# Sliding-window attention and a token-mixing MLP: PSUM as eight single banks, each with reads of its own

## The chip, the cores and the metric

The kernel runs on one core of a Trainium2 chip. The metric is device time in microseconds (us), the median of three runs. The core has a matrix engine (TensorE, PE in the profile; PEld is its weight load), a vector engine (VectorE, DVE), a scalar engine (ScalarE, ACT), GpSimd (POOL) and a sync engine (SP). Each works through its own list of instructions in order, and waits at an instruction until what it needs is there. PE writes its results only to PSUM, a small memory of eight banks, each 128 partitions by 512 fp32 numbers; ACT and DVE read PSUM and write SBUF, the working memory. In this kernel POOL starts nearly all input transfers, SP and ACT the output transfers.

## The reference

Eight batches, eight heads, 576 tokens, head size 64. Attention with a linear distance penalty, over the last 128 tokens, then a token-mixing MLP on the concatenated heads:

```python
scores = scale * np.matmul(q, k.transpose(0, 1, 3, 2))
mask = (rel >= 0) & (rel < 128)
scores = np.where(mask, scores - slopes * np.abs(rel), -1e9)
attn = softmax(scores)
x = np.matmul(attn, v)                      # then heads side by side: (8, 576, 512)
wq = x @ w_q; wk = x @ w_k                  # 512 -> 64
W_tok = einsum('bsd,btd->bst', wq, wk) / 8
mixed = einsum('bst,btd->bsd', W_tok, x)
out = np.maximum(mixed, 0) @ w_out          # 512 -> 512
```

## The kernel before

The program is a list of named operations. A long string, `ORDER`, gives their order and the engine of each (`:P` PE, `:A` ACT, `:D` DVE, `:G` POOL, `:S` SP) and, for PE, the PSUM place. It is written out by hand or by a tool outside the file; nothing decides about the order at run time. Every engine gets the operations that name it, in the order of the string.

The operations of one batch `b`, in the order in which data passes through them:

- `Lq`, `Lk`, `Lv`, `Lt` load q, k, v and the last 64 tokens (POOL). `LF` loads the first pieces of batch 0 in fp32 (ACT, SP).
- `TQ`, `TK`, `TT`, `TJ`, `TF` transpose q and k on PE into PSUM; `ETQ`, `ETK`, `ETT`, `EJ`, `EF` copy the results to the tile `qkT` (L252 on ACT, L254 on DVE).
- `QK b.g.u` makes the scores of key block `g` (0 to 3) and head half `u`: four heads, 1024 numbers in each partition, which is two banks. `EXP b.g.u` (L657, ACT) takes the exponential of the 1024 into the tile `pt`. `MUL b.g` (L672, DVE) multiplies the 2048 numbers of both halves with the penalty and mask factors in `bias`.
- `PV b.t` multiplies with v for query block `t`, with the row sums in a 65th column for each head, for all eight heads into two banks. `RC` (L723, DVE) takes the reciprocals of the eight sums, `X` (L733, DVE) scales the 512 numbers into the tile `x`. Block 4 holds the last 64 tokens and takes one bank (L720, L727).
- `XT b.i` transposes two blocks of `x` (L243), eight transposes of 128x128 into one bank, and `EXT` copies the 1024 fp16 numbers to `xT`. `XTT`, `EXTT` do the last 64 tokens.
- For each pair of batches: `WQ`, `WK`, `WT` (products with w_q and w_k), `G` (wk times x), `MX 0..4` (the mixed tokens, two banks each), `RM` and `RMT` (relu, L886 on ACT, L888 on DVE), `OUT` (product with w_out, four matmuls of 512 columns), `EO` (copy to the staging tile `osb`), `DO` (store).
- `WM` are matmuls on zeros, put where PE would pause; `WARM` has their numbers. `wmc` and `bias` make the factors at the start, `zeros`, `ones` and `pads` clear tiles.

PSUM is four tiles `pair0` to `pair3` of two banks. An operation of two banks takes a whole pair (`:P2`), one of one bank half a pair (`:P21`). The function `apart` declares that operations on the two banks of one pair don't depend on each other; an operation that reads both banks at once holds both until it is done.

Of the kernel before, what the change touches and what calls it, by code (L numbers as in the profile page):

```python
# [8 lines left out]
FP32 = mybir.dt.float32  # L9
# [8 lines left out]
H = 8  # L18
# [20 lines left out]
LOGB = ()  # L39

LAST = (7, 3)

PAIRED = 9
# [3 lines left out]
WARM = (6, 9, 1, 1, 2, 3,)  # L47

ORDER = """
warm:D LF0.0.0.0:A LF0.0.1.0:S ones.2:D iota:G LF0.0.1.1:A LF0.1.0.0:S ident:G LF0.0.0.1:A  # L50
zeros:D LF0.1.0.1:S Lv2.4:G ones.1:D Lq0.2:G pads:D Lk0.2:G wmc:D WM.0:P31 TF0.0.0:P00 Lk0.1:G
ones.3:D bias:A Lq1.0:G ones.0:D TF0.0.1:P01 idh:D Lk1.0:G TF0.1.1:P10 EF0.0.1:D Lk1.1:G
TF0.1.0:P11 EF0.1.1:D Lv0.0:G EF0.0.0:A EF0.1.0:A Lk1.2:G Lk1.3:G WM.1:P31 TJ0.2.1:P1
QK0.0.1:P0 QK0.0.0:P2 EJ0.2.1:D Lv0.1:G TJ0.2.0:P30 EXP0.0.0:A TJ0.1.1:P1 EJ0.2.0:D Lk0.3:G
EXP0.0.1:A QK0.2.1:P3 EJ0.1.1:D QK0.2.0:P2 QK0.1.1:P1 EXP0.2.1:A MUL0.0:D TQ1:P0 EXP0.2.0:A
Lv0.2:G QK0.1.0:P3 Lt0:G ETQ1:D EXP0.1.0:A TK1.0:P2 ETK1.0:D EXP0.1.1:A Lv1.0:G MUL0.2:D
WM.2:P01 QK1.1.1:P2 QK1.1.0:P3 QK1.0.1:P1 EXP1.1.1:A Lv1.1:G QK1.0.0:P0 MUL0.1:D EXP1.1.0:A
Lq2.0:G TK1.1:P2 ETK1.1:D EXP1.0.1:A Lk2.3:G PV0.0:P3 QK1.2.1:P2 RC0.0:D Lk2.2:G X0.0:D
EXP1.0.0:A PV0.1:P1 MUL1.1:D PV0.2:P3 Lv1.2:G EXP1.2.1:A QK1.2.0:P0 Lv0.3:G RC0.1:D EXP1.2.0:A
X0.1:D TT0:P2 RC0.2:D Lv1.3:G TJ0.3.1:P1 X0.2:D ETT0:A XT0.0:P00 ETT1:A MUL1.0:D Lk2.0:G  # L60
EJ0.3.1:A WM.3:P01 QK1.3.0:P2 Lv0.4:G EXP1.3.0:A EXT0.0:D PV1.0:P1 QK0.3.1:P3 RC1.0:D PV1.1:P0
X1.0:D EXP0.3.1:A QK0.3.0:P2 MUL1.2:D QK1.3.1:P1 EXP0.3.0:A TQ2:P3 Lk2.1:G RC1.1:D EXP1.3.1:A
MUL0.3:D Lv1.4:G ETQ2:A WM.4:P21 TK2.1:P1 X1.1:D Lt1:G ETK2.1:D PV1.2:P2 XT1.0:P00 RC1.2:D
PV0.3:P3 X1.2:D Lw1:G QK2.2.1:P1 MUL1.3:D Lk3.1:G EXP2.2.1:A Lw0:G RC0.3:D WM.5:P01 PV1.3:P2
EXT1.0:A X0.3:D Lq3.0:G PV0.4:P01 RC1.3:D X1.3:D TK2.0:P3 QK2.2.0:P1 Lv2.0:G RC0.4:D PV1.4:P00
ETK2.0:D EXP2.2.0:A XT1.1:P20 Lk3.0:G RC1.4:D X0.4:D QK2.0.0:P3 EXT1.1:D XT0.1:P21 EXP2.0.0:A
Lk3.3:G QK2.0.1:P1 X1.4:D EXT0.1:D QK2.1.1:P0 Lk3.2:G EXP2.0.1:A TT2:P3 QK2.1.0:P2 ETT2:D
Lv2.1:G EXP2.1.1:A ETT3:D WK0:P10 MUL2.0:D Lv2.2:G EXP2.1.0:A XTT0:P0 QK2.3.0:P3 EXTT0:D
WQ0:P11 Lv2.3:G EWK0:A MUL2.1:D EXP2.3.0:A QK2.3.1:P0 TQ3:P2 Lq4.0:G MUL2.2:D EXP2.3.1:A Lwo0:G
WT0:P10 ETQ3:D PV2.0:P0 EWT0:A Lwo1:G TK3.0:P3 ETK3.0:A G0:P10 RC2.0:D Lk4.1:G X2.0:D MUL2.3:D  # L70
# [12 lines left out]
TK4.1:P3 OUT0.3:P21 EXP5.0.0:A Lk6.0:G ETK4.1:D TT4:P1 EO0.0:D EO0.3:A Lq6.02:G XTT2:P3
QK5.1.1:P0 ETT5:D ETT4:A OUT1.0:P20 EXTT2:D Lk6.2:G EXP5.1.1:A MUL4.1:D PV4.0:P3 Lk6.1:G
QK4.2.0:P1 EO1.0:A QK4.2.1:P0 RC4.0:D WK2:P21 EXP4.2.0:A X4.0:D Lv5.1:G MUL5.1:D OUT1.4:P20
EXP4.2.1:A Lk6.3:G PV4.1:P1 MUL5.0:D EWK2:A Lq6.01:G EO1.4:A TK5.1:P0 QK4.3.0:P3 Lv4.3:G
WQ2:P21 RC4.1:D EXP4.3.0:A X4.1:D Lq6.00:G ETK5.1:D WT2:P20 EWQ2:A QK4.3.1:P3 MUL4.2:D EWT2:A
Lq6.03:G QK5.2.0:P0 PV5.0:P1 EXP4.3.1:A G2:P20 Lk7.0:G RC5.0:D X5.0:D EXP5.2.0:A Lv4.4:G
MUL4.3:D QK5.2.1:P3 XT4.0:P21 EG2:A Lk7.1:G PV4.2:P0 EXP5.2.1:A EXT4.0:D MX2.3:P1 Lq7.02:G
RC4.2:D MX2.2:P2 RM2.3:A X4.2:D TK6.1:P3 Lt3:G ETK6.1:D TK6.0:P0 RM2.2:A PV5.1:P1 ETK6.0:D  # L90
MX2.0:P3 RC5.1:D PV4.3:P0 Lq7.01:G X5.1:D RM2.0:A QK5.3.1:P2 RC4.3:D TQ6:P1 Lv5.2:G X4.3:D
# [68 lines left out]
def kernel(  # L160
# [45 lines left out]
    def one(bank):  # L206
        return pairs[bank[0]][:, bank[1], :]
# [867 lines left out]
```

## Time and profile before

| | before |
|---|---|
| median of 3 runs | 137.24 us (136.44 to 137.88) |
| span of the profiled execution, first to last instruction | 135.4 us |
| PE busy | 122.8 us (91%), 2174 matmuls |
| DVE busy | 114.0 us (84%), 197 instructions |
| ACT busy | 107.3 us (79%), 145 instructions |
| POOL busy | 86.3 us (64%), 108 instructions |
| granted TensorE clock | 1.000 |

The profile gives the profiled execution's span, not its device time; the median lies 1.84 us above the span. Times of a row are microseconds from the span's start. On ACT and DVE an instruction's end overlaps the next one's start, so that the time from start to start in an unbroken sequence, called the step below, is shorter than an instruction's duration. A row of the timeline that covers several instructions (x12) gives their time together. In the view of waits a row names who waited, for whom, how long in all, how often and the longest.

### The profile page before, as it was taken

The page shows a single profiled execution, that of the slowest core. Times are in us where ns is not written, and L with a number is a line of the kernel's source. Part 1 is how long each engine was busy: PE and PEld are TensorE (multiplying, and loading weights), DVE is VectorE, ACT ScalarE, POOL GpSimd, SP SyncE. Part 2 cuts the span into 40 slices and gives each one's busy share as a digit, 9 for nine tenths or more (in the row PEclk, how much of TensorE's full clock was granted, in tenths as well). Part 3 has the DMA queues.
Part 4 walks back from the last instruction along what each step waited for, and adds up shares of the span by engine and source line. Part 5 has one row for each costly group of instructions (what it writes and reads, how often), then busy time and mean ns, then how long its engine had stood idle before and what let it go on. Part 6 is the DMA issues. An engine that isn't in the chain of part 4 may idle for free.

```text
span 135.4 us, 5054 instructions
## 1 busy us (share of the span) xinstructions
PE 122.8 (91%) x2174; PEld 78.1 (58%) x2174; DVE 114.0 (84%) x197; ACT 107.3 (79%) x145; POOL 86.3 (64%) x108
## 2 busy tenths in 40 slices
PE   6598867889999799999999999999999999999970
PEld 2264546666676476575566576565685576634440
DVE  5733899999999999998999999699999999557830
ACT  2574999995999999998999999999999962367040
POOL 7998979599979759899999999997000000000000
PEclk9999999999999999999999999999999999999999
DMA  4999999999999999999999999999999900858894
GB/s 106 211 165 169 155 156 180 165 158 154 167 159 163 195 184 153 157 154 157 155 157 158 152 153 155 151 185 258 269 223 348 331 14 5 258 185 328 264 368 151
DMA packets 105414, 24.97 MB, mean 184 GB/s; under 512 B 95536, under 2 KB 100912, under 8 KB 105392
## 3 DMA queue, kind: packets, MB, share of 16 engines
q0 software_dynamic: 96832, 14.42, 150.2%
q1 hardware_dynamic: 6688, 9.44, 20.4%
q10 hardware_dynamic: 1872, 0.79, 2.2%
q8 instruction: 17, 0.28, 0.8%
q14 instruction: 5, 0.04, 0.1%
HBM read 29.62 MB, written 9.44 MB: 288 GB/s over the span
## 4 chain that ended last, share of the span: by engine, by line
PE 67%; DVE 13%; ACT 10%; DMA 3%; issue 3%; ACTq 1%; DVEq 0%
PE pair L240 54%; PE pair L243 12%; ACT pt L657 6%; DVE pt L672 4%; DVE qkT L254 4%; DMA osb<-in_q_dram 3%; DVE x L733 3%; ACT qkT L252 2%; DVE rm L888 1%; ACTq L412 1%; ACT rm L886 1%; DVE inv L723 1%; ACT wqT L252 0%; DVE xT L254 0%; ACT gs L252 0%
## 5 line engine op out<-in xcount | busy, mean ns | idle before, releaser
L657 ACT ACTIVATE pt<-pair 128x1024 f16<-128x1024 f32 x64 | 62.8, 1038 | 6.5 <-PE pair L240 5.9
L672 DVE TENSOR_TENSOR pt<-pt,bias 128x2048 f16<-128x2048 f16 x32 | 38.5, 1217 | 0.4 <-ACT pt L657 0.3
L393 POOL DMA_DIRECT2D vt<-in_v_dram x40 | 35.3, 968 | 1.1 <-issue 0.5
L240 PE MATMUL pair<-wout_sb,rm 128*128 128x512 f16 (+1 forms) x132 | 31.7, 373 | 0.0
L367 POOL DMA_DIRECT2D natk<-in_k_dram x31 | 28.6, 947 | 2.9 <-DMA natq<-in_q_dram 1.6
L240 PE MATMUL pair<-vt,pt 128*128 128x65 f16 (+1 forms) x576 | 21.9, 194 | 1.9 <-DVE rm L888 0.5
L240 PEld LDWEIGHTS <-pt 128*128 128x128 f16 (+1 forms) x576 | 19.1, 100 | 7.6 <-issue 3.4
L240 PE MATMUL pair<-qkT 64*128 64x256 f16 (+2 forms) x320 | 22.3, 250 | 1.3 <-DVE qkT L254 0.8
L254 DVE COPY qkT<-pair 128x1024 f16<-128x1024 f16 (+2 forms) x27 | 19.3, 734 | 4.1 <-PE pair L243 3.9
L733 DVE TENSOR_TENSOR x<-pair,inv 128x512 f16<-128x512 f32 x32 | 21.8, 690 | 0.9
L252 ACT COPY osb<-pair 128x512 f32<-128x512 f32 (+1 forms) x24 | 14.0, 596 | 10.5 <-PE pair L240 9.7
L240 PEld LDWEIGHTS <-rm 128*128 128x128 f16 x132 | 11.4, 97 | 12.1 <-issue 2.2
L240 PEld LDWEIGHTS <-qkT 64*128 64x128 f16 x320 | 11.1, 94 | 8.6 <-issue 5.4
L254 DVE COPY osb<-pair 128x512 f32<-128x512 f32 (+1 forms) x13 | 8.7, 668 | 5.1 <-PE pair L240 5.1
L379 POOL DMA_DIRECT2D natq<-in_q_dram x12 | 11.5, 995 | 2.2 <-PE pair L240 1.6
L886 ACT ACTIVATE rm<-pair 128x1024 f16<-128x1024 f32 x11 | 11.1, 1045 | 0.5 <-PE pair L240 0.3
L243 PE MATMUL pair<-identh,x 128*128 128x128 f16 x128 | 9.8, 220 | 0.0
L240 PE MATMUL pair<-warm 128*128 128x512 f16 x22 | 7.8, 491 | 1.5 <-DVE warm L295 1.2
L243 PEld LDWEIGHTS <-x 128*128 128x128 f16 x128 | 7.6, 98 | 2.3 <-issue 1.2
L254 DVE COPY xT<-pair 128x1024 f16<-128x1024 f16 x11 | 7.5, 685 | 1.2 <-PE pair L243 1.1
L243 PE MATMUL pair<-identh,natk 64*128 64x64 f16 x248 | 6.5, 191 | 1.2 <-ACT pt L657 0.9
L243 PEld LDWEIGHTS <-natk 64*128 64x128 f16 x248 | 5.3, 94 | 3.9 <-issue 3.3
(68 smaller groups left out, 136.2 us busy)
## 6 DMA issues: line engine op xcount, KB each, us to landing
out_dram<-osb SPq DMA_DIRECT2D x30, 256.0 KB, 3.5
vt<-in_v_dram POOLq DMA_DIRECT2D x32, 128.0 KB, 7.2
natk<-in_k_dram POOLq DMA_DIRECT2D x31, 128.0 KB, 5.8
natq<-in_q_dram POOLq DMA_DIRECT2D x4, 512.0 KB, 7.7
natq<-in_q_dram POOLq DMA_DIRECT2D x12, 128.0 KB, 5.7
out_dram<-osb SPq DMA_DIRECT2D x9, 128.0 KB, 2.5
vt<-in_v_dram POOLq DMA_DIRECT2D x8, 64.0 KB, 5.7
natt<-in_q_dram POOLq DMA_DIRECT2D x4, 128.0 KB, 5.7
```

Source lines behind the costliest of these rows:

```text
L240: hold(nc.tensor.matmul(*a, **k))
L243: hold(nc.tensor.transpose(*a))
L252: hold(nc.scalar.copy(out_ap, in_ap))
L254: hold(nc.vector.tensor_copy(out=out_ap, in_=in_ap))
L367: return lambda: nc.gpsimd.dma_start(out=natk(b, n), in_=k[b, :, P * n:P * n + P, :].transpose([1, 0, 2]))
L379: return lambda: nc.gpsimd.dma_start(out=rows_q(b)[:, r], in_=q[b, :, 0:512, :].rearrange("h (p r) d -> r p h d", r=QR)[r])
L393: return lambda: nc.gpsimd.dma_start(out=vtv(b, t)[:n, :, 0:D], in_=v[b, :, P * t:P * t + n, :].transpose([1, 0, 2]))
L412: (nc.scalar if o.eng == "ACT" else nc.sync).dma_start(out=nat32(j, n)[:, 4 * u:4 * u + 4, :], in_=(q, k)[j][0, 4 * u:4 * u + 4, P * n:P * ...
L657: nc.scalar.activation(out=pt, in_=two(hold_.bank).rearrange("p e c -> p (e c)"), func=AF.Exp, scale=SCALE)
L672: nc.vector.tensor_tensor(out=pv, in0=pv, in1=bt, op=ALU.mult)
L733: nc.vector.tensor_tensor(out=x_s[b % NX][qt].rearrange("p (g h d) -> p g h d", g=2, h=4), in0=sums(p)[:, :, :, 0:64], in1=box["inv"].unsq ...
L886: hold(nc.scalar.activation(out=out_ap, in_=in_ap, func=AF.Relu, scale=WSCALE))
```

## The change

PSUM becomes eight tiles of one bank. An operation of two banks now names any two of them (`:P13` is banks 1 and 3), and `apart` is gone, since banks are tiles of their own. Every read that took two banks at once is now two reads, named `a` and `b`, one for each bank, which may run on different engines and at different places:

- `EXP`: two exponentials of 512 for each of 64 units, 128 in place of 64.
- `PV`, `RC`, `X`: four heads each, so 64 of each in place of 32 for the full blocks.
- `RM`, `RMT`: one relu for each bank.
- `ETQ`, `ETK`, `ETT`, `EJ`, `EXTT`: one copy for each bank.
- `XT`: sixteen transposes of 64x64 blocks on row halves of PE into two banks (as `TK` did before) in place of eight of 128x128 into one, and so two copies `EXT`.

`MUL`, `QK`, `OUT`, the loads and the stores keep their sizes. `WARM` grows from 22 to 37 matmuls in ten places. `ORDER` is new throughout. Code for an unused variant of the penalty (`LOGB`) goes.

```diff
-WARM = (6, 9, 1, 1, 2, 3,)
+WARM = (7, 3, 3, 6, 5, 1, 1, 2, 5, 4,)
...
-QK0.0.1:P0 QK0.0.0:P2 EJ0.2.1:D Lv0.1:G TJ0.2.0:P30 EXP0.0.0:A TJ0.1.1:P1 EJ0.2.0:D Lk0.3:G
+EF0.1.1:A Lt0:G EF0.1.0:A QK0.0.0:P13 TJ0.2.0:P2 EXP0.0.0a:A EXP0.0.0b:A TJ0.1.1:P04 EJ0.2.0:D
...
-    pairs = [ppool.tile([P, 2, 512], FP32, name=f"pair{i}") for i in range(4)]
-    def one(bank):
-        return pairs[bank[0]][:, bank[1], :]
-    def two(bank):
-        return pairs[bank[0]]
+    banks = [ppool.tile([P, 512], FP32, name=f"bank{i}") for i in range(8)]
+    def one(bank, r=0):
+        return banks[bank[r]]
+    def oneh(bank, r=0):
+        return banks[bank[r]].bitcast(F16)
...
-        def ex(o):
-            nc.scalar.activation(out=pt, in_=two(hold_.bank).rearrange("p e c -> p (e c)"),
-                                 func=AF.Exp, scale=SCALE)
+        x = []
+        for e in range(2):
+            def ex(o, e=e):
+                nc.scalar.activation(out=pt[:, 512 * e:512 * e + 512], in_=one(s.bank, e), func=AF.Exp, scale=SCALE)
+            x.append(add("EXP", b, f"{g}.{u}{'ab'[e]}", w + 0.6, {"ACT": (0.92, 1.02)}, [s, *oldp], ex,
+                         frees=[s], half=e))
...
-            for h in range(H):
+            px = one(o.bank)
+            for h in range(4 * o.half_, 4 * o.half_ + 4):
...
-                box["inv"] = spool.tile([P, 2, 4], FP32, name="inv", tag="inv", bufs=6)
-                nc.vector.reciprocal(out=box["inv"], in_=sums(p)[:, :, :, 64])
+                box["inv"] = spool.tile([P, 4], FP32, name="inv", tag="inv", bufs=12)
+                nc.vector.reciprocal(out=box["inv"], in_=sums(p)[:, :, 64])
...
-                    if b >= PAIRED:
-                        tp2(o, 2 * c + n, x, x)
-                    else:
-                        tp(oneh(o.bank)[:, 256 * c + P * n:256 * c + P * n + P], x, identh)
+                    tp2(o, len(its) * c + n, x, x)
...
-                relu(o.eng, rm_s[pr % 2][:, db].rearrange("p r e (t x) -> p (e t) r x", t=4),
-                     two(t.bank).rearrange("p e (t r x) -> p (e t) r x", t=4, r=QR))
+            for h in range(2):
+                def ev(o, h=h):
+                    relu(o.eng, rm_s[pr % 2][:, db, :, h, :].rearrange("p r (t x) -> p t r x", t=4),
+                         one(t.bank, h).rearrange("p (t r x) -> p t r x", t=4, r=QR))
```

The new order shows at three places. First DVE at the start, where `warm`, `wkt`, `vt` and `qkT` are tiles that are cleared and `wm` is the source of the factors `bias`. Before:

```order
1 L295 MEMSET warm 128x256
2 L321 MEMSET vt_96 64x264
3 L322 MEMSET vt_96 128x40
4 L326 MEMSET qkT_76 128x8x32
5 L326 MEMSET qkT_77 128x8x32
...
11 L331 MEMSET wkt_133 64x2x32
12 L316 TENSOR_SCALAR wm<-wint 128x384
13 L317 SCALAR_TENSOR_TENSOR wm<-wint,wm 128x384
14 L318 SCALAR_TENSOR_TENSOR wm<-wm,wint 128x384
```

The same place on DVE now, with the same tiles:

```order
1 L287 MEMSET warm 128x256
2 L308 TENSOR_SCALAR wm<-wint 128x384
3 L309 SCALAR_TENSOR_TENSOR wm<-wint,wm 128x384
4 L310 SCALAR_TENSOR_TENSOR wm<-wm,wint 128x384
5 L313 MEMSET vt_92 64x264
6 L314 MEMSET vt_92 128x40
```

The three operations that make `wm` have moved ahead of the ten that clear tiles.

Second, DVE past the middle of the program, with the reciprocals (`inv`), the scaled products (`x`), the multiply with the factors (`pt`) and copies of transposes (`qkT`, `xT`). Before:

```order
76 L723 RECIPROCAL inv<-pair_143 128x8
77 L733 TENSOR_TENSOR x_114<-pair_143,inv 128x512
78 L672 TENSOR_TENSOR pt_98<-pt_98,bias 128x2048
79 L723 RECIPROCAL inv<-pair_142 128x8
80 L733 TENSOR_TENSOR x_115<-pair_142,inv 128x512
```

A place in the middle on DVE now, with the same kinds of tile:

```order
121 L712 TENSOR_TENSOR x_115<-bank_138,inv 128x256
122 L712 TENSOR_TENSOR x_112<-bank_140,inv 128x256
123 L707 RECIPROCAL inv<-bank_145 128x4
124 L658 TENSOR_TENSOR pt_98<-pt_98,bias 128x2048
125 L707 RECIPROCAL inv<-bank_139 128x4
126 L263 COPY qkT_74<-bank_141 128x4x2x64
127 L712 TENSOR_TENSOR x_115<-bank_145,inv 128x256
```

Reciprocals and products are of half the size and twice as many, and something else often stands between a reciprocal and its product.

Third, ACT around the last exponential, with relus (`rm`, `rmt`), copies for the stores (`osb`) and of transposes (`xT`, `xTt`). Before:

```order
118 L657 ACTIVATE pt_98<-pair_143 128x1024
119 L252 COPY osb<-pair_141 128x512
120 L886 ACTIVATE rmt_138<-pair_142 128x2x4x64
121 L886 ACTIVATE rm_136<-pair_140 128x8x4x32
122 L252 COPY osb<-pair_141 128x512
123 L252 COPY xTt_127<-pair_143 128x512
124 L886 ACTIVATE rm_136<-pair_142 128x8x4x32
```

The same place on ACT now:

```order
210 L646 ACTIVATE pt_97<-bank_142 128x512
211 L261 COPY xT_122<-bank_145 128x4x2x64
212 L261 COPY xT_122<-bank_143 128x4x2x64
213 L261 COPY osb<-bank_139 128x512
214 L261 COPY osb<-bank_141 128x512
215 L261 COPY osb<-bank_144 128x512
216 L865 ACTIVATE rmt_136<-bank_140 128x4x64
```

Before, the large relus of the third pair of batches (`rm_136`) come behind the last exponential, and now they are done ahead of it; with them, six of that pair's nine `OUT` moved ahead of it too.

472 lines of the change are left out of this document (229 added, 243 removed).

## The prediction

> **What bounds the kernel now.** I read the page first: the busy times, then the slices.
>
> ```profile
> PE 122.8 (91%) x2174; PEld 78.1 (58%) x2174; DVE 114.0 (84%) x197; ACT 107.3 (79%) x145; POOL 86.3 (64%) x108
> PE   6598867889999799999999999999999999999970
> DVE  5733899999999999998999999699999999557830
> ACT  2574999995999999998999999999999962367040
> ```
>
> PE is the busiest by the share, but from slice 7 to 33 DVE and ACT also stand at nines. A busy PE is not a PE at its peak, since its matmuls are pipelined, so I don't take the 91% for a bound. The program has three stages: a head until the first exponential, a middle from the first to the last, and a tail. The view by windows gives the middle for ACT (first to last exponential) and for DVE (first to last multiply), and the part of the tail from `WK6` on.
>
> ```profile
> core 0: us, PE busy (x) PEld busy (x) DVE busy (x) ACT busy (x) POOL busy (x), PEclk, DMA share, GB/s
> 12.02:105.41 93.39, 87.68 (x1855) 59.33 (x1855) 89.05 (x143) 88.89 (x116) 75.03 (x89) 1.00 2.15 179
> 13.99:109.03 95.04, 89.89 (x1872) 60.22 (x1867) 91.50 (x146) 90.32 (x119) 73.57 (x87) 1.00 2.10 183
> 116.28:135.40 19.12, 15.04 (x121) 7.29 (x119) 8.99 (x13) 6.65 (x10) 0.00 (x0) 1.00 0.76 261
> ```
>
> In their middles ACT is busy 88.89 of 93.39 us and DVE 91.50 of 95.04. Little idle time is left for finer reads to remove. The view of waits says which of it PSUM could cause:
>
> ```profile
> ACT pt L657 <- PE pair L240: 5.9, 8, 2.8
> DVE qkT L254 <- PE pair L243: 5.1, 5, 2.9
> PE pair L243 <- ACT pt L657: 1.1, 4, 0.4
> PE pair L240 <- ACT pt L657: 0.9, 3, 0.5
> ```
>
> PE waited for exponentials to empty PSUM for 2.0 us in all. The two longest waits of ACT and DVE, 2.8 and 2.9 us, lie in the head. So the middle is bound by the work of ACT and DVE, and the question is what the change adds to it.
>
> **Steps.** In an unbroken sequence an instruction costs its step, from start to start. For ACT:
>
> ```profile
> 5.12 3.41 ACT L336 ACTIVATE bias<-wm 128x384 f16<-128x384 f32 x8 [1.40 <-DVE wm L318]
> 12.02 11.17 ACT L657 ACTIVATE pt<-pair 128x1024 f16<-128x1024 f32 x12 [2.75 <-PE pair L240]
> 59.23 0.59 ACT L886 ACTIVATE rmt<-pair 128x512 f16<-128x512 f32 x1
> 59.70 0.59 ACT L252 COPY osb<-pair 128x512 f32<-128x512 f32 x1
> ```
>
> Twelve exponentials of 1024 in 11.17 us, the last of which lasts about 1.03: step 0.92. A relu of 512: 59.70 - 59.23 = 0.47. The trace has no exponential of 512. Its low end is that relu, 0.47; its high end comes from the eight of 384, (3.41 - 0.51) / 7 = 0.41, and a line through 384 and 1024: 0.51. I take the middle, 0.49. If the overlap were lost, it would be the duration, 0.59. For DVE:
>
> ```profile
> 38.92 2.36 DVE L672 TENSOR_TENSOR pt<-pt,bias 128x2048 f16<-128x2048 f16 x2
> 57.18 0.28 DVE L723 RECIPROCAL inv<-pair 128x8 f32<-128x8 f32 x2
> 60.45 0.69 DVE L733 TENSOR_TENSOR x<-pair,inv 128x512 f16<-128x512 f32 x1
> 61.05 0.20 DVE L723 RECIPROCAL inv<-pair 128x8 f32<-128x8 f32 x1
> 61.29 0.69 DVE L733 TENSOR_TENSOR x<-pair,inv 128x512 f16<-128x512 f32 x1
> 63.20 0.42 DVE L727 TENSOR_TENSOR xtl<-pair,invt 128x256 f16<-128x256 f32 x1
> 63.54 0.68 DVE L254 COPY xT<-pair 128x1024 f16<-128x1024 f16 x1
> 64.14 1.22 DVE L672 TENSOR_TENSOR pt<-pt,bias 128x2048 f16<-128x2048 f16 x1
> 66.47 0.41 DVE L254 COPY qkT<-pair 128x512 f16<-128x512 f16 x1
> 66.80 0.41 DVE L254 COPY xTt<-pair 128x512 f16<-128x512 f16 x1
> ```
>
> Multiply 2.36 - 1.22 = 1.14; product `X` of 512 0.60 (61.05 - 60.45), of 256 0.34 (63.54 - 63.20); fp16 copy of 1024 0.60, of 512 0.33. Two halves thus cost 0.07 more than one whole. An fp16 copy of 256 is an estimate, half the slope below: 0.20. A reciprocal costs 0.08 when another follows (0.28 - 0.20), but 0.24 when its own product does (61.29 - 61.05), so 0.16 of stall; a half of four saves none of it.
>
> **The change, part by part: the middle.** Counts are from the two orders, between the first and last exponential (multiply).
>
> ACT before: 64 exponentials x 0.92 = 58.9; ten other reads of 1024 x 0.92 = 9.2; one of 2048 at 1.8; 31 of 512 x 0.47 = 14.6; nine small 1.3. Sum 85.8, in a stage of 93.4. ACT after: 128 halves x 0.49 = 62.7; eight of 1024 = 7.4; 59 of 512 x 0.47 = 27.7; seven of 256 x 0.27 = 1.9 (0.27 estimated with the same slope); three small 0.4. Sum 100.1. Of the 14.3 us added, 3.8 are the split exponentials; most of the rest are copies of `qkT` and `xT` and relus, which are more in number, taken over from DVE, or done ahead of the last exponential now.
>
> DVE before: 32 multiplies x 1.14 = 36.5; nine more reads at 1.14 = 10.3; 53 at 0.60 = 31.8; 15 at 0.33 = 5.0; 36 reciprocals x 0.08 = 2.9, and 31 stalls x 0.16 = 5.0. Sum 91.5, in a stage of 95.0. After: 36.5; 24 at 0.60 = 14.4; 95 at 0.33 = 31.4; 28 at 0.20 = 5.6; 64 reciprocals = 5.1; 39 stalls = 6.2. Sum 99.2. So DVE gets 7.7 more, and ACT becomes the fuller of the two.
>
> The Trainium skill (Perfetto Trace Analysis, "Optimizing Scalar/DVE Operations") puts the overhead of one read of PSUM at about 51 ns on ScalarE and 125 on VectorE, and advises grouping where the engine is saturated, which speaks against this change. By its 125 ns, some 60 ns above the 67 of the rows, the 113 PSUM reads of DVE before would make its load 98.1 us, more than the 95.0 that the stage lasted, so the trace decides for 67; with 211 such reads after, DVE's load by the page would be 111.9 us, and the time near 148.
>
> Before, the fuller engine (DVE) took 95.0 us for 91.5 of steps, 1.038 times its load. I take the same factor for ACT after: 100.1 x 1.038 = 103.9 us. Ends: no loss and halves at 0.47, 97.5; ACT's own factor from before, 93.4 / 85.8, 109.0.
>
> **The head.**
>
> ```profile
> 2.43 1.28 ACT L336 ACT_TABLE_LOAD   x1 [2.43 <-issue]
> 3.61 0.29 DVE L316 TENSOR_SCALAR wm<-wint 128x384 f32<-128x384 int32 x1
> 8.40 2.92 PE L240 MATMUL pair<-warm 128*128 128x512 f16 x9
> 8.44 0.83 ACT L252 CAST qkT<-pair 128x512 f16<-128x512 f32 x2
> ```
>
> Nine warm-up matmuls (2.92 us, 0.32 each) stood between the first transposes and the first scores; now three do, which saves 1.9. On ACT the factors `bias` (5.12 to 8.53) stood ahead of the first copies (8.44). `wm` moves ahead of the tile clears on DVE, so `bias` can begin when the table load ends at 3.71, 1.4 earlier, and doesn't replace PE as the cause. The first exponential comes at about 9.8 in place of 12.02. Ends: 9.0, and 12.0 if the loads decide. On POOL's queue a v load that was issued first now waits, and q and k go ahead; both sides of that are inside these ends.
>
> **PE** is covered in the middle:
>
> ```profile
> 106.00 0.62 PE L243 MATMUL pair<-identh,x 128*128 128x128 f16 x8
> 18.66 0.41 PE L243 MATMUL pair<-identh,natk 64*128 64x64 f16 x16 [0.37 <-ACT pt L657]
> ```
>
> A transpose group of `x` falls from 0.62 to the 0.41 of the same form on `natk`: 16 x 0.21 = 3.4 us less, against 15 more warm-ups x 0.32 = 4.8, which stand where PE would pause. I cost both at nothing, as ACT and DVE hide them; if that cover were gone they'd cost 1.4.
>
> **The tail.**
>
> ```profile
> 104.28 1.13 ACT L657 ACTIVATE pt<-pair 128x1024 f16<-128x1024 f32 x1
> 107.81 1.22 DVE L672 TENSOR_TENSOR pt<-pt,bias 128x2048 f16<-128x2048 f16 x1
> 116.28 1.10 PE L240 MATMUL pair<-wqk_sb,xT 128*128 128x64 f16 x32
> 124.24 7.08 PE L240 MATMUL pair<-wout_sb,rm 128*128 128x512 f16 x36
> ```
>
> Before, `WK6` starts 10.9 us after the last exponential, and 19.1 us remain: 30.0. After, between the last exponential and `WK6` there are the last multiply (1.2) and on DVE nine products x 0.33, eight reciprocals x 0.08 with four stalls, two copies x 0.33, and the last one's write: about 5.4. So 6.6. From `WK6` on, four `OUT` stood before the final ones; now one does. One is four matmuls of 7.08 / 36 = 0.20, so 0.8; of the 2.4 us I take 1.7, since some of it filled PE's waits. 17.4 remain, the tail is 24.0. Ends: 22.5, and 25.7.
>
> **Sum.** 9.8 + 103.9 + 24.0 = 137.7 us of span, 2.3 over the 135.4. The median lies 137.24 - 135.4 = 1.84 above the span, so 139.5; I say 140, as the ends reach further up than down.
>
> **The rivals.** *The waits go, and it is faster.* Banks come free by halves, PE runs further ahead, and ACT works without a gap at 0.47 for a half: 9.8 + 97.5 + 24.0 + 1.84 = 133.1 us. It decides below about 100 us for the middle. For it: the 5.9 and 5.1 us of waits, the shorter tail, and 2.0 us of PE's waits. Against: it needs two engines, loaded 98 to 99 us each, that never miss each other, where now the fuller loses 3.8%. The skill's page has this as a rule too (same section): breaking instructions up may let work finish sooner where ACT and DVE aren't saturated; here the slices show them saturated.
>
> *It comes out even.* Half the loss goes: 9.8 + 100.1 x 1.019 + 24.0 + 1.84 = 137.6.
>
> *The overlap goes.* Each half waits for a matmul or a bank of its own, and a third of the 128 exponentials cost 0.59: 4.3 us more, and if the loads hold the first exponential at 12.0, 2.2 more: 146.0.
>
> **How the numbers follow.** A measurement here tells about 1% from no change, so faster means below 135.9 and slower above 138.6. Chances: the forecast 0.53, faster 0.20, even 0.16, overlap lost 0.11. The range takes in the nearer half of the faster case, down to 133.5, and most of the last, up to 146.5; left out are the far ends of these two. Faster 0.20, same 0.16, slower 0.64.
>
> **What would show it.** The step of an exponential of 512: 0.49, between 0.47 and 0.59. ACT and DVE at nines until about 113 us; last exponential at about 114 us, not 105; first at about 10. Waits of PE for ACT below 2.0 us. The tail from the last exponential 24 us. I'm wrong if ACT's middle takes under 100 us, which its load forbids unless halves cost less than 0.47, or if PE, with more `OUT` in the middle, becomes what ACT waits for.

## The result and the profile after

The kernel after takes 144.22 us (median of 4, 143.02 to 145.15), the kernel before 137.56 in the same comparison (136.44 to 138.28): 1.049 times as long, with an interval of 1.041 to 1.057. The profiled execution, the longest of the four, took 145.15 us with a span of 143.4. In all that follows the ratios leave out slow executions, over 1.5% above the fastest of the same kernel, while the medians count them, and the profiles of e1, e5 and e6 are of such a one (151.13, 144.27 and 146.08 us).

First the page of the kernel after: busy times, then the slices of four rows.

```profile
PE 127.8 (89%) x2317; PEld 80.3 (56%) x2317; DVE 117.1 (82%) x298; ACT 121.7 (85%) x244; POOL 86.2 (60%) x108
DVE  5615879997997999999578999999999999936730
ACT  3938899999989999999669999999999998948230
POOL 8995987895999579992590999999800000000000
PEclk9978999999999999999779999999999999999997
```

ACT has 14.4 us more work than before and DVE 3.1, as expected of smaller reads and of copies that moved to ACT. On ACT the nines last through slice 32, counted from 0, which is 118 us at 3.6 us a slice; before they lasted through slice 31 of 3.4 us, 108 us. But there is a hole that no step of the prediction has: about slice 20 DVE, ACT, POOL and the granted clock dip together.

The timeline of ACT at three places in the middle:

```profile
10.72 1.08 ACT L646 ACTIVATE pt<-bank 128x512 f16<-128x512 f32 x2 [1.44 <-PE bank L625]
23.61 4.16 ACT L646 ACTIVATE pt<-bank 128x512 f16<-128x512 f32 x8
116.98 2.18 ACT L646 ACTIVATE pt<-bank 128x512 f16<-128x512 f32 x4
```

The view by windows from the first exponential to the end of the last (columns as in the prediction: the stretch, its length, the busy time of PE, PEld, DVE, ACT and POOL, the granted clock, the DMA share and GB/s):

```profile
10.72:119.16 108.44, 101.55 (x2016) 65.98 (x2017) 98.68 (x245) 103.44 (x206) 76.23 (x90) 0.98 1.98 183
```

| | predicted | measured |
|---|---|---|
| first exponential | 9.8 | 10.7 |
| middle | 103.9 | 108.4 |
| tail from the last exponential | 24.0 | 24.2 |
| span | 137.7 | 143.4 |

The middle carries 4.5 of the 5.7 us that are missing in the span, the head 0.9. In the middle ACT's busy time grew by 14.6 us, from 88.89 to 103.44, nearly what the prediction's sum adds (14.3); what grew beyond it is idle time. The view by windows around the hole:

```profile
66.00:72.00 6.00, 4.27 (x122) 3.21 (x120) 4.21 (x14) 4.68 (x11) 2.18 (x3) 0.84 2.30 155
72.00:78.00 6.00, 5.88 (x94) 3.34 (x93) 4.60 (x11) 4.65 (x10) 3.08 (x4) 0.87 2.27 167
```

POOL's timeline there, with its waits in brackets:

```profile
69.82 0.87 POOL L349 DMA_DIRECT2D natk<-in_k_dram  x1 [4.07 <-DMA natt<-in_k_dram]
78.80 1.76 POOL L361 DMA_DIRECT2D natq<-in_q_dram  x2 [3.72 <-PE bank L532]
```

ACT loses 2.7 of 12 us and DVE 3.2 here, while POOL, which issues the loads, waits twice: 4.1 us for earlier loads to land, then 3.7 us for PE, which must finish the transposes `TQ5` before the q tile can be filled again.

ACT and DVE wait for PE here, and PE itself waits for no load between 64 and 80 us. Its timeline has a pause within a row of transposes, for which the profile names no cause, and soon after it a group of matmuls that runs slowly:

```profile
69.30 0.29 PE L257 MATMUL bank<-identh,x 64*128 64x64 f16 x7 [1.44 <-issue]
70.81 1.89 PE L804 MATMUL bank<-wqk_sb,xT 128*128 128x64 f16 x32
```

The trace's record of the granted clock is 0.5 from 70.1 to 73.6 us; the same group takes 1.11 us at 101.75. The pause follows PE's 2241st instruction. In the traces of this kernel and its variants, every pause of PE over 0.4 us without a named cause follows an instruction whose number leaves 193 when divided by 256, and the page's instruction queue moves 18 packets, 0.29 MB, which is 16 KB for about 256 of PE's 4644 instructions. So PE probably waited for its next block of instructions. The queue's eighth packet, the next one at this place, landed 1.2 us before PE went on, and 1.4 in e6 below, which pauses here too; in e5 and e7, which hold the stores back, it landed 3.3 and 1.8 us before PE came to the place, and there is no pause. That the stores delayed the packet fits this, but is not shown.

SP's timeline shows what else is new among the loads, the stores. Of the kernel before, its first row; of the kernel after, its first three:

```profile
88.11 15.37 SPq L993 DMA_DIRECT2D out_dram<-osb  x12
```

```profile
51.54 0.36 SPq L971 DMA_DIRECT2D out_dram<-osb  x1
56.80 1.18 SPq L974 DMA_DIRECT2D out_dram<-osb  x2
59.87 43.11 SPq L971 DMA_DIRECT2D out_dram<-osb  x12
```

Before, the first store in SP's list was `DO3.3`, which is ready late, and so all stores waited until 88 us, when nearly all loads had been issued. The new order puts `DO1.1` first, and stores run from 51 us on, among the loads.

### The profile page after: what moved, and what is told of

It is laid out like the page before. It is cut to its first block, busy times and chain, and to the rows that moved or that the text cites. A ratio compares the mean times of both kernels' runs of the same rounds, so it can differ in the third digit from the quotient of the medians.

```text
span 143.4 us, 5543 instructions
## 1 busy us (share of the span) xinstructions
PE 127.8 (89%) x2317; PEld 80.3 (56%) x2317; DVE 117.1 (82%) x298; ACT 121.7 (85%) x244; POOL 86.2 (60%) x108
## 2 busy tenths in 40 slices
DMA packets 105417, 25.00 MB, mean 174 GB/s; under 512 B 95536, under 2 KB 100912, under 8 KB 105392
## 3 DMA queue, kind: packets, MB, share of 16 engines
q0 software_dynamic: 96832, 14.42, 143.2%
## 4 chain that ended last, share of the span: by engine, by line
PE 49%; ACT 22%; DVE 16%; issue 6%; DMA 4%; SPq 1%; ACTq 0%; DVEq 0%
PE bank L953 17%; ACT pt L646 16%; PE bank L625 7%; DVE pt L658 5%; PE bank L257 5%; DVE x L712 5%; PE bank L685 4%; DMA osb<-in_q_dram 4%; PE bank L292 3%; DVE inv L707 2%; PE bank L804 2%; PE bank L848 2%; DVE qkT L263 2%; ACT qkT L261 1%; PE bank L536 1%
## 5 line engine op out<-in xcount | busy, mean ns | idle before, releaser
L646 ACT ACTIVATE pt<-bank 128x512 f16<-128x512 f32 x128 | 70.9, 679 | 3.4 <-PE bank L625 3.2
L953 PE MATMUL bank<-wout_sb,rm 128*128 128x512 f16 x124 | 30.4, 379 | 0.4 <-ACT pt L646 0.2
L712 DVE TENSOR_TENSOR x<-bank,inv 128x256 f16<-128x256 f32 x64 | 24.9, 416 | 0.6
L625 PE MATMUL bank<-qkT 64*128 64x256 f16 (+2 forms) x320 | 24.0, 256 | 0.9 <-ACT pt L646 0.2
L685 PEld LDWEIGHTS <-pt 128*128 128x128 f16 x448 | 16.9, 97 | 6.9 <-issue 2.2
L263 DVE COPY qkT<-bank 128x256 f16<-128x256 f16 (+2 forms) x45 | 16.2, 397 | 5.6 <-ACT pt L646 3.1
L261 ACT COPY osb<-bank 128x512 f32<-128x512 f32 (+1 forms) x26 | 16.8, 674 | 4.6 <-PE bank L953 4.3
L685 PE MATMUL bank<-vt,pt 128*128 128x65 f16 x448 | 19.6, 193 | 0.5 <-DVE pt L658 0.3
L261 ACT COPY qkT<-bank 128x512 f16<-128x512 f16 (+2 forms) x20 | 15.8, 808 | 0.3 <-PE bank L536 0.3
L292 PE MATMUL bank<-warm 128*128 128x512 f16 x37 | 11.8, 447 | 1.5 <-DVE warm L287 1.2
L707 DVE RECIPROCAL inv<-bank 128x4 f32<-128x4 f32 x72 | 10.2, 167 | 0.3 <-PE bank L685 0.2
```

What stands on the lines that cost most here:

```text
L261: nc.scalar.copy(out_ap, in_ap)
L263: nc.vector.tensor_copy(out=out_ap, in_=in_ap)
L292: mm(one(o.bank), warm[:, 0:P], warm, start=True, stop=True)
L625: mm(one(o.bank, e)[:, 256 * a + c0:256 * a + c0 + wd], t[r, 1, hp, P * kb:P * kb + P], t[r, 0, hp, q0:q0 + wd], start=True, stop=True)
L646: nc.scalar.activation(out=pt[:, 512 * e:512 * e + 512], in_=one(s.bank, e), func=AF.Exp, scale=SCALE)
L685: mm(px[:, 65 * (h % 4):65 * (h % 4) + 65], ptc(kb, h, cur, P), vtv(b, kb)[:, h, 0:65], start=(i == 0), stop=(i == len(kbs) - 1))
```

## The experiments

Times are medians; "before" is the kernel before on the same chip. Line numbers are those of each kernel.

### Stores in other places, and the reads alone

**e1**: the kernel after, with eight stores behind `DO2.3`, so that they start at 81 us.

```diff
-... EO1.1:A MX0.4:P46 Lk4.0:G QK2.3.1:P17 DO1.1:S RMT0.b:D ...
+... EO1.1:A MX0.4:P46 Lk4.0:G QK2.3.1:P17 RMT0.b:D ...
...
+... EO2.3:A DO2.3:S DO1.0:S DO1.1:S DO0.3:S DO0.1:S DO1.4:S DO0.0:S DO0.2:S DO1.3:S Lq6.02:G
```

> The changed kernel, with the first eight stores put behind the store of OUT2.3 on SP (so at about 82 us and no longer from 51 us on); nothing else. Theory O (the new order lets stores run among the loads, loads land late, PE, DVE and ACT find a hole at 66 to 78 us and the granted clock falls there): the hole goes, 3 to 4 us less, ratio to the kernel before 1.015 to 1.03, clock near 1.0. Theory S (the halves alone fill ACT and DVE): the hole is not what bounds it, ratio stays at 1.04 to 1.05.

**e2**: the kernel before, with nine stores directly behind their copies, so that stores start at 54 us.

```diff
-... EO0.2:A QK3.2.0:P1 ...
+... EO0.2:A DO0.2:S QK3.2.0:P1 ...
```

> The kernel before, with the nine stores of the first pair of batches right behind their copies on SP, so from about 53 us on in place of 88; nothing else. Theory O: loads land late between 55 and 75 us and the kernel gets 2 to 4 us slower, ratio 1.015 to 1.03. Theory S: stores cost nothing, ratio 0.995 to 1.005.

**e3**: the kernel before, with each read of two banks as two reads back to back, in the same order. **e4**: the same for the exponentials alone.

```diff
-            nc.scalar.activation(out=pt, in_=two(hold_.bank).rearrange("p e c -> p (e c)"), ...)
+            for e in range(2):
+                nc.scalar.activation(out=pt[:, 512 * e:512 * e + 512], in_=two(hold_.bank)[:, e, :], ...)
```

> The kernel before with its pairs, its order and its engines, but each read of two banks made as two reads back to back: exponentials, reciprocals and products, copies, relus. Theory S: DVE gets 32 x 0.07 (products) + 32 x 0.08 (reciprocals) + 47 x 0.07 (copies, relus) = 8 us more and ACT about 5, in stages where DVE had 3.5 us to spare and ACT 7.6: ratio 1.035 to 1.06. Theory O: the halves cost little by themselves, ratio under 1.015.

> The kernel before with each exponential of 1024 made as two of 512 back to back; nothing else. Theory S: 64 x 0.06 = 3.8 us more on ACT, which had 7.6 us to spare while DVE is the fuller: ratio 1.005 to 1.025. If halves lost their overlap (0.59 in place of 0.49), 64 x 0.26 = 17 us more and ratio 1.06 or above. Theory O: under 1.01.

Before took 137.40 us. Measured:

| | us | ratio to before, interval |
|---|---|---|
| e1 | 149.48 | 1.084 (1.076 to 1.092) |
| e2 | 143.27 | 1.043 (1.036 to 1.050) |
| e3 | 141.39 | 1.028 (1.022 to 1.034) |
| e4 | 139.99 | 1.019 (1.013 to 1.024) |

e2 is the strongest: nothing but the place of nine stores, and the kernel before loses 5.9 us, more than the 2 to 4 expected. Its slices show a hole on DVE, from slice 17 to 25:

```profile
DVE  5624899999999999988686888699999999557730
```

and in its waits PE stands for a load:

```profile
PE pair L242 <- DMA natk<-in_k_dram: 2.1, 2, 1.7
ACT osb L251 <- DMA out_dram<-osb: 4.6, 1, 4.6
```

The second row, a copy that stands until a store has freed a staging tile, lies at 130 us and costs little: the stretch behind the last exponential takes 30.2 us, and 30.0 before.

In e3 the reads alone cost 4.0 us, a ratio between its two expected ranges; 2.6 of them are the exponentials (e4). The half exponentials in e4's timeline, and then in e3's with its last ones:

```profile
13.07 11.87 ACT L658 ACTIVATE pt<-pair 128x512 f16<-128x512 f32 x24 [3.81 <-PE pair L240]
```

```profile
12.12 11.86 ACT L663 ACTIVATE pt<-pair 128x512 f16<-128x512 f32 x24 [2.85 <-PE pair L240]
107.87 1.25 ACT L663 ACTIVATE pt<-pair 128x512 f16<-128x512 f32 x2
```

With 0.59 for the last of them the step is (11.87 - 0.59) / 23 = 0.49. e3's middle is 109.1 - 12.1 = 97.0 us, 3.6 more than before.

e1 went the other way than a theory of early stores asks: 5 us worse than the kernel after. Its waits say why:

```profile
POOL natq L360 <- PE bank L531: 7.5, 1, 7.5
PE bank L256 <- DMA natk<-in_k_dram: 5.1, 1, 5.1
```

The wait for loads at 66 us went, but POOL then came to its q loads earlier and stood 7.5 us for `TQ5`; the loads behind it slid into the stores that now start at 81 us, and PE waited 5.1 us for a k tile. Moving the stores to 81 us moved the late loads and did not cure them.

### The stores and the q loads, each and together

**e5**: the kernel after, with 20 staging tiles and the first nine stores held until `EO2.2`. **e6**: with a third q tile. **e7**: both (18 staging tiles). **e8**: the edits of e2 and e3 together in the kernel before.

```diff
-NQ = 2
+NQ = 3
-OSB = 14
+OSB = 18
...
+... EO2.2:A DO2.2:S DO1.1:S DO1.4:S DO0.0:S DO1.0:S DO0.1:S DO1.3:S DO0.2:S DO0.3:S DO3.3:S ...
```

> The kernel after with 20 staging tiles in place of 14, and all of the first nine stores held until EO2.2 is copied, so that no store starts before about 95 us, when all but a few loads are issued. Theory S (the part of the 6.7 us that the prediction missed is stores that move among the loads and slow them): the loads end about 5 us earlier than in the kernel after (issue of the last at 98 to 100 us, not 104), the last exponential ends at 114 to 116 in place of 119.2, and the time is 139 to 141.5 us. Theory W (it is the q loads that stand on POOL behind TQ5, and PE's pause there at 66 to 78 us, whatever the stores do): the 3.7 us wait of POOL for PE stays or grows, the last load is issued at 103 or later and the time stays at 143 to 146. Theory L (neither: two reads for one simply lose more than the factor 1.038 in such a middle): loads may end early, but the last exponential stays at 118 to 120 and the time at 143 to 145.

> The kernel after with a third q tile (NQ 3 in place of 2), in the same order: the q loads of batches 6 and 7 no longer wait for TQ5 and its neighbours to free the tile. Stores stay where they are. Theory W: the 3.7 us wait of POOL for PE goes, the hole at 72 to 78 us closes, and the time falls to 139.5 to 142. Theory S: the wait goes, but the loads still meet the stores; the time falls by less than 1.5 us, to 142.7 or more. Theory L: unchanged, 143.5 to 145.

> Both of the two edits before: three q tiles, and the first nine stores held until EO2.2 is copied (18 staging tiles). What is left is the kernel after with neither early stores nor q loads that wait for PE. Theories S and W together: the last load is issued by 97 us, the middle falls to about the predicted 103.9 us, and the time is 138 to 140.5 us. Theory L: the loads run ahead and nothing follows from it; 142 to 145 us.

> The kernel before with both of two edits that were run apart: all reads of two banks as two reads back to back (alone 141.4 us, 4.0 over before), and nine stores directly behind their copies, from about 53 us on (alone 143.3 us, 5.9 over). If the two costs add, as they would where ACT and DVE are full and loads come late in other stretches: 146 to 148.5 us. If the late loads merely give ACT and DVE idle time in which the added reads are done, the larger hides part of the smaller: 143.5 to 146 us, near the kernel after's 144.2.

| | us (range) | ratio to before (137.57), interval |
|---|---|---|
| e5 | 143.12 (141.5 to 144.3) | 1.034 (1.024 to 1.044) |
| e6 | 144.84 (141.8 to 147.0) | 1.035 (1.022 to 1.048) |
| e7 | 141.60 (140.1 to 142.2) | 1.023 (1.013 to 1.033) |
| e8 | 144.08 (143.8 to 145.3) | 1.047 (1.038 to 1.055) |

Each edit alone leaves POOL a long wait at the same place. Its timeline in e5, with the stores out of the way:

```profile
78.11 1.76 POOL L354 DMA_DIRECT2D natq<-in_q_dram  x2 [6.29 <-PE bank L525]
```

and in e6, with the wait for PE out of the way:

```profile
71.34 0.88 POOL L375 DMA_DIRECT2D vt<-in_v_dram  x1 [4.81 <-DMA vt<-in_v_dram]
```

POOL's waits do not open the hole by themselves, though. Between 66 and 82 us ACT is idle 2.7 us in the kernel after and 2.6 in e6, where the stores stay; it is idle 0.4 us in e5, where they are held and POOL waits longest, and 0.2 in e7. The profiled execution of e5 lost its time in the head instead: from 10 to 22 us ACT is busy 8.2 us, in e6 8.4, in the kernel after 10.1 and in e7 10.2 (the last section comes back to this). By the times alone it isn't shown what either edit is worth, since the intervals of e5 and e6 overlap both that of the kernel after and that of e7.

With both edits POOL's timeline has no wait from 50 us on, and the windows of e7 show the hole closed and the middle 2.7 us shorter:

```profile
10.66:116.37 105.71, 99.91 (x2016) 65.44 (x2017) 98.66 (x245) 103.22 (x206) 76.34 (x90) 0.99 2.01 187
66.00:72.00 6.00, 5.62 (x160) 4.23 (x162) 5.56 (x17) 5.84 (x13) 6.00 (x8) 1.00 2.43 156
72.00:78.00 6.00, 5.71 (x120) 3.50 (x117) 5.89 (x13) 6.00 (x12) 6.00 (x8) 1.00 2.44 156
```

The time falls from 144.2 to 141.6, not into the expected 138 to 140.5. As a ratio the forecast, 140 over 137.24, is 1.020, and that lies inside e7's interval. e8 fits the forecast in which costs overlap: 5.9 and 4.0 alone, 6.5 together.

### The head

**e9**: e7 with `WARM` 9, 1, 1, 1 in place of 3, 3, 6, 5 from the second place on. **e10**: with 3, 1, 1, 1. **e11**: the kernel before, with three warm-ups ahead of the first scores. **e12**: the kernel before, with a head in which PE hardly pauses (`wmc` first, one more group of four warm-ups, two in place of nine ahead of the first scores, `pads` and `Lv2.4` later).

```diff
-WARM = (6, 9, 1, 1, 2, 3,)
+WARM = (6, 2, 1, 1, 2, 3, 4,)
...
-... pads:D Lk0.2:G wmc:D WM.0:P31 TF0.0.0:P00 Lk0.1:G ...
+... iota:G wmc:D LF0.0.1.1:A ... WM.0:P31 TF0.0.0:P00 WM.6:P31 Lk0.1:G ...
```

> The kernel of e7 (the kernel after without early stores, three q tiles) with nine warm-up matmuls ahead of the first scores, as before the change, and one each in place of 3, 6 and 5 between the first score groups. Theory P (PE runs at half its rate until it has been busy for some 4 us without a pause; with three warm-ups it is still at that rate when the scores begin, and the 14 warm-ups between them are work on the path): four score matmuls take 0.39 from the start and not 0.61, the first exponential comes at about 12.0 and not 10.7, but ACT then runs on without gaps to 22 us; time 139.5 to 141.5 us, the same or up to 2 us less than e7's 141.6, with less scatter between runs. The prediction's reading (warm-ups only fill pauses of PE; six of them saved 1.9 us): the first exponential is 1.9 later and so is the end, 143 to 144 us.

> As e9, but with three warm-ups ahead of the first scores as in the kernel after, so that only the 11 warm-ups between the score groups are taken out. Theory P: PE stays at half its rate longer, since it now pauses between the score groups (four score matmuls at 0.61 beyond 17 us), and what the missing warm-ups free is lost again: 141.5 to 143.5 us. The prediction's reading (they lie in PE's pauses and cost nothing): 141 to 142 us, PE at the full rate as in e7. If the 11 warm-ups were merely work on the path (11 x 0.24 = 2.6 us): 139 to 140 us.

> The kernel before with one number changed: three warm-ups ahead of the first scores in place of nine. This is the prediction's term 'saves 1.9' by itself. If the term holds, the first exponential comes at 10.6 to 11.0 and the time is 135.7 to 136.7 us. Theory P: the first exponential comes earlier by some 1 us, but score groups and transposes take 1.5 times as long until about 16 us, ACT waits for PE there, and the time is 137 to 138.5 us: nothing gained.

> The kernel before with a head that keeps PE busy: wm is made first on DVE (so that bias is done 1.4 us earlier on ACT), four warm-ups stand in PE's pause at 4.9 to 6.6 us, two in place of nine ahead of the first scores, and one v load is issued behind the first k loads. Theory P: PE, busy from 1.2 us on, is at its full rate by about 7 us, the first exponential comes at 9.3 to 10.2 in place of 12.0 and ACT runs on; the middle moves ahead by as much unless the loads (last issue at 94 us, DMA full until then) hold it: 135.3 to 136.6 us. Rival (the loads bound the middle of the kernel before, so that a shorter head gains nothing): 137 to 138 us.

| | first exponential | us (range) | ratio to before (137.75), interval |
|---|---|---|---|
| e9 | 10.9 | 143.05 (141.4 to 143.5) | 1.038 (1.031 to 1.044) |
| e10 | 10.2 | 141.89 (141.5 to 142.8) | 1.032 (1.027 to 1.037) |
| e11 | 10.5 | 137.45 (136.8 to 139.2) | 0.998 (0.994 to 1.002) |
| e12 | 9.8 | 137.95 (137.4 to 138.5) | 1.003 (1.000 to 1.005) |

e11 is the prediction's term "saves 1.9" by itself: the first exponential does come 1.5 us earlier than at 12.0, and within the interval nothing of it reaches the end. In its profiled execution the granted clock is 0.54 from 20 to 27 us, so this trace can't tell what took the lead. e12, whose clock stays at 1.00 there, gives 2.2 us at the start, and nothing at the end either. The exponentials at the same places in the two timelines, before and then e12:

```profile
24.71 3.98 ACT L657 ACTIVATE pt<-pair 128x1024 f16<-128x1024 f32 x4
35.12 3.77 ACT L657 ACTIVATE pt<-pair 128x1024 f16<-128x1024 f32 x4 [0.17 <-PE pair L240]
```

```profile
9.79 3.77 ACT L649 ACTIVATE pt<-pair 128x1024 f16<-128x1024 f32 x4 [0.82 <-PE pair L232]
23.68 3.77 ACT L649 ACTIVATE pt<-pair 128x1024 f16<-128x1024 f32 x4
35.18 3.77 ACT L649 ACTIVATE pt<-pair 128x1024 f16<-128x1024 f32 x4 [0.17 <-PE pair L232]
```

The lead of 2.2 us is 1.0 at 24 us and gone at 35. PE's timeline in e12 shows where it goes, in waits for q, k and v:

```profile
21.62 0.40 PE L235 MATMUL pair<-identh,natt 64*128 64x64 f16 x15 [0.64 <-DMA natt<-in_k_dram]
26.28 1.08 PE L235 MATMUL pair<-identh,natq 128*64 128x128 f16 x32 [0.69 <-DMA natq<-in_q_dram]
28.83 0.61 PE L232 MATMUL pair<-vt,pt 128*128 128x65 f16 x15 [0.34 <-DMA vt<-in_v_dram]
```

The theory in e9's and e10's expectations, that fewer warm-ups keep PE at a low rate for longer and so cost time, found no support: e9, with nine of them, was not faster than e7, and in e10's profile PE is at the higher rate from 9.8 us on. e10's 141.9 us lies in two of the ranges that were expected of it.

### Cheaper loads

**e13** to **e16**: the k loads as one piece of 2 KB for each partition, in before, e12, after and e10.

```diff
-            out=natk(b, n), in_=k[b, :, P * n:P * n + P, :].transpose([1, 0, 2]))
+            out=natk(b, n).rearrange("p h d -> p (h d)"),
+            in_=k[b, :, :, :].rearrange("h t d -> (h t d)")[65536 * n:65536 * n + 65536]
+            .rearrange("(p x) -> p x", p=P))
```

> The kernel before with the k loads of POOL taken as 512 neighbouring numbers for each partition (2 KB in one piece, not eight pieces of 256 bytes). The k that is loaded is then k's numbers in another arrangement, so the output is not the reference's; bytes, instructions and waits are otherwise the same. Theory D (the stream of loads, 155 GB/s in 256-byte packets until 94 us, sets the pace of the middle before): the last load is issued 10 us or more earlier, PE's waits for DMA go, and the time falls by 1.5 to 4 us, to 133.5 to 136. Theory L (the middle before is bound by ACT and DVE, as the prediction had it): the loads end earlier and the time stays within 0.7 us of before, 137 to 138.

> The kernel of e12 (before, with a first exponential at 9.8) with the same wider k loads. Theory D: now the 2.2 us of the shorter head reach the end: 1 to 2.2 us less than e13. Rival (the head is lost to something else): the same as e13 within 0.5 us.

> The kernel after with the same wider k loads; stores stay among the loads and the q loads behind TQ5. Theory D: the stream has room for the stores, POOL's waits for DMA fall from 10 us to under 4, the hole at 66 to 78 us closes, the last exponential ends at 114 to 116 and the time falls from 144.2 to 139.5 to 141.5. Theory L: 143 to 145.

> The kernel of e10 (after, with three q tiles, no early stores, fewer warm-ups) with the same wider k loads. There the loads were out of the way already and ACT stood at 9.9 of 10 us from 40 us on, so the two theories agree that little is left to gain: 139.5 to 142 us. A fall to under 139 would say that the loads still held ACT in that kernel, and that ACT's work alone takes less than the 105 us of its middle.

| | us (range) | ratio to before (137.87), interval |
|---|---|---|
| e13 | 137.86 (136.4 to 139.0) | 0.998 (0.994 to 1.003) |
| e14 | 137.04 (136.0 to 139.6) | 0.993 (0.988 to 0.997) |
| e15 | 144.94 (142.1 to 148.8) | 1.036 (1.027 to 1.044) |
| e16 | 140.91 (140.4 to 141.5) | 1.025 (1.019 to 1.032) |

POOL's last issues, before and in e13, and the first exponentials in e13:

```profile
86.33 7.79 POOL L393 DMA_DIRECT2D vt<-in_v_dram  x9
```

```profile
81.40 7.62 POOL L395 DMA_DIRECT2D vt<-in_v_dram  x9
11.82 11.17 ACT L659 ACTIVATE pt<-pair 128x1024 f16<-128x1024 f32 x12 [2.54 <-PE pair L240]
```

The loads end 5 us earlier and the time stays: theory D fell for the kernel before. Its middle is bound by ACT and DVE, as the prediction had it, and its loads, as they are, don't hold it up. In e14 a part of the shorter head seems to count, where in e12 it did not. The timeline of e14 has its first and last exponentials at:

```profile
10.32 11.18 ACT L651 ACTIVATE pt<-pair 128x1024 f16<-128x1024 f32 x12 [0.82 <-PE pair L232]
102.86 1.13 ACT L651 ACTIVATE pt<-pair 128x1024 f16<-128x1024 f32 x1
```

1.5 us ahead of e13 at the start, 1.1 at the last exponential (103.96 there), 0.8 in the median. That is less than the 1 to 2.2 us that theory D expected, and the intervals of e13 and e14 overlap.

e16 is the kernel after with everything out of the way. Its first exponential comes at 9.64 us, and its view by windows gives the middle almost as forecast:

```profile
9.64:114.47 104.83, 97.13 (x2005) 64.38 (x2005) 98.61 (x245) 103.17 (x206) 68.07 (x90) 1.00 1.69 189
```

e15 keeps stores and q loads where they are; its ratio was 1.4 hundredths below that of the kernel after, with intervals that overlap, and its runs scatter from 142.1 to 148.8, so its time settles little. Its profiled execution (142.13 us) has no hole: ACT is idle 0.5 us between 66 and 82, though POOL waits 3.7 us for a load and 3.9 for PE there.

**e17** and **e18** ask whether the head can be had with the reference's computation: e12 with the q loads of batches 5 to 7 as one of 512 KB each (`LATEQ` 8), and the same with three q tiles.

```diff
-LATEQ = 5
+LATEQ = 8
...
-... Lq5.01:G ... Lq5.02:G ... Lq5.03:G ... Lq5.00:G
+... Lq5.0:G
```

> The kernel of e12 (before, with a first exponential at 9.8) with the q loads of batches 5 to 7 taken like those of batches 1 to 4: one load of 512 KB in pieces of 1 KB for each, at the place of the first of the four 128 KB loads in pieces of 256 bytes. The computation is the reference's. It takes 9 of 108 issues from POOL and 9,216 of 96,832 packets from the stream, but only from batch 5 on, after 45 us, while e12 lost its lead to loads before 35 us. If only the stream's load in total decides: 136.3 to 137.3 us, like e14's 137.0. If it is the stream in the first 35 us that decides: 137.3 to 138.2 us, like e12.

> As e17, with a third q tile, so that a 512 KB load needn't wait until the transposes of the batch two before it are done. If e17 is held by POOL waiting behind such a load, this is faster than e17 by 0.5 us or more; if not, the same as e17 within 0.5 us.

139.36 us (138.7 to 140.4), 1.009 times before (1.005 to 1.012), and 139.06 (138.4 to 141.8), 1.007 (1.004 to 1.011): above e12 (1.003), though the intervals still touch, and neither case of e17's expectation had that. The third q tile brought 0.3 us, which its expectation takes for no gain. POOL's timeline in e17 has a new wait behind a large load:

```profile
59.25 0.82 POOL L378 DMA_DIRECT2D natt<-in_q_dram  x1 [3.47 <-DMA natq<-in_q_dram]
```

No version that computes the reference was faster than the kernel before by more than its interval.

## Why the prediction was right in direction and too small

**Right.** The half exponential: forecast step 0.49; 0.49 in e4, and (4.16 - 0.60) / 7 = 0.51 in the kernel after. The overlap is not lost. The tail: 24.0 forecast, 24.2 measured. ACT becomes the fuller engine: 103.4 us busy in the middle against 98.7 of DVE, and the work that the sum adds to it, 14.3 us, is there (14.6, and 14.3 in e16). The premise that the middle before is bound by ACT and DVE held against cheaper loads (e13). And the middle's load, 100.1 us times 1.038 = 103.9, was a good figure for ACT and DVE alone: in e16 the middle takes 104.8, the whole span 138.6 against the 137.7 of the sum.

**Wrong.** The step that failed is the size of the middle: "Before, the fuller engine (DVE) took 95.0 us for 91.5 of steps, 1.038 times its load. I take the same factor for ACT after". The factor was 108.4 / 100.1 = 1.083; with the stores and q loads out of the way 105.7 / 100.1 = 1.056 (e7), and with cheaper loads and fewer warm-ups as well 104.8 / 100.1 = 1.047 (e16). The transfer of the factor took the loads to stay covered. Before, the stores came behind nearly all loads, and POOL's q loads waited for PE only 1.6 us in all. The new order moved both, and the prediction, which followed ACT, DVE and PE from row to row, gave SP's and POOL's queues no term in the middle. The 103.9 us would have left ACT 0.5 us idle beside its 103.4 us of work. It was idle for 5.0 us, 2.7 of them in the hole; in e7 for 2.5, in e16 for 1.7, and before for 4.5. The upper end of the forecast, ACT's own factor from before (109.0), comes near the measured 108.4, but it stood for other idle time than that of the hole: that is luck. The row of DMA slices on the page of the kernel before was the place to ask whether there is room for stores among the loads:

```profile
DMA  4999999999999999999999999999999900858894
```

It stands at nines from slice 1 to 31, until 108 us. POOL issues loads for the first 94 of these, and from 88 us on the stores take their place.

**How the 6.7 us divide.** The division is a rough one, since costs of the two kinds overlap in e8. What the smaller reads and the new order cost without load troubles is 3 to 4 us: 3.0 between e16 and e13, both with cheap loads (140.9 - 137.9), and 4.0 in e3, where the reads alone were split. The stores and q loads together are the other 2 to 3: 144.2 against 141.6 (e7) and 141.9 (e10). The intervals of e7 (up to 1.033) and e10 (up to 1.037) lie below that of the kernel after (from 1.041). That of e9, which has the same two edits and more warm-ups, overlaps it and gives 1.2, so the size of this part is uncertain.

**The head** was mis-sized by 0.9 (9.8 forecast, 10.7 measured); 0.3 of it is in the sum itself, as 12.02 - 1.9 is 10.1. Its gain was taken at full price where it was worth nothing: e11 and e12 start the exponentials 1.5 and 2.2 us earlier and end level, e9 and e10 start 0.7 apart, and their last exponentials end 0.1 apart (115.7 and 115.6). In e12 the early start runs into loads that are not there yet.

**The warm-ups** were costed at nothing. e9 has six more of them than e10 and took 1.2 us longer, with intervals that overlap; that they cost nothing isn't shown.

**The rivals.** "The waits go" did not happen: the middle needed more than 100 us in each variant of the kernel after. "The overlap goes" gave a time near the measured one, 146.0, for a reason that the steps of 0.49 to 0.51 rule out.

**Two smaller slips.** ACT does not stand at nines from slice 7 to 33 before: its row has a 5 in slice 9, and a 6 and a 2 in slices 32 and 33. DVE's load of 111.9 us is 111.4 with the 58 ns for each read that give the 98.1 beside it. Neither changes the forecast.

**Open.** Why the runs of e6 and e15 scatter (141.8 to 147.0 and 142.1 to 148.8) was not tried; those of the kernel after, e2 and e8, with stores among the loads too, lie within 2.2 us each. It isn't shown either how much of the hole is PE's pause and how much the lower clock behind it, or whether the stores bring on the pause, and how.

## What to carry to other kernels

When a change writes a new order, compare the list of every queue, the stores' and loads' too: here nine stores in other places alone cost 5.9 us, and splitting every read 4.0. A gain in one stage counts only as far as the next stage's inputs are there to use it; ask which transfer would be late if the stage began earlier. When an edit doesn't show in the time, look in its trace whether the idle time that it aimed at has gone: in e5 the hole was closed, and the time was lost in the head. A long wait of the engine that issues the loads need not be the cause: look for what the full engines wait for, and then for what that one waits for.

## What the runs showed of the hardware

**Stores among small loads.** In the kernel before the loads keep the DMA engines at nines with 161 GB/s between 20 and 90 us, mostly in packets under 512 bytes (95,536 of 105,414); nine stores among them cost 5.9 us (e2). With k in pieces of 2 KB the same bytes took 69,056 packets in place of 96,832 on the loads' queue, and POOL was busy 76.4 us, not 86.3.

**PE's rate in the head.** PE's timeline in the kernel after, in e10, and in e7 and e5 further on:

```profile
10.08 0.61 PE L625 MATMUL bank<-qkT 64*128 64x256 f16 x4
```

```profile
9.75 0.39 PE L618 MATMUL bank<-qkT 64*128 64x256 f16 x4
```

```profile
12.88 0.61 PE L618 MATMUL bank<-qkT 64*128 64x256 f16 x8
```

```profile
13.87 1.03 PE L618 MATMUL bank<-qkT 64*128 64x256 f16 x8
```

The same scores take 0.39 or 0.61 us for four, 0.61 or 1.03 for eight, from one profiled execution to the next, and e7 and e5 have the same head. The traces' records of the granted clock go with it: 0.5 from 8.7 to 12.1 us in the kernel after and from 8.4 to 11.8 in e7, then 1.0; in e10 1.0 from the first record on, at 9.6 us. In e5 the first record comes only at 16.5 us. The column reads 1.00 ahead of it, where the rows are slow, so a 1.00 there is no measurement. The stretches at 0.5 in the head and in the middle of the kernel after last 3.41 us each. The Trainium skill (TensorE: Matmul & The Clock Gate, "What's actually happening") describes a half rate until PE has been busy for a window of about 3.4 us that runs freely, and calls the point of change variable from run to run; these rows and records agree with it. What it costs is open: e10, with the higher rate from 9.8 us on, took 141.9 us and e7 141.6, but in the profiled executions of e5 and e6, where eight scores still take 1.03 us at 13.7 to 13.9 us, ACT is busy 1.7 to 2.0 us less up to 22 us than in the kernel after and in e7.
